# Splitting w2 by rows over fewer partitions, and a jump ahead in VectorE's program, in a decode step of attention and a feed-forward layer

## The chip, the cores and the metric

The kernel runs on one core of one Trainium2 chip. A core has five engines that run their own programs and meet at semaphores: TensorE (PE, matrix multiplication), VectorE (DVE), ScalarE (ACT), GpSimd (POOL) and SyncE (SP, which here only issues transfers). Sixteen DMA engines move data between the chip's memory (HBM) and the core's on-chip memory (SBUF, 128 partitions). The results of TensorE go to a second on-chip memory, PSUM. The metric is the device time of one execution in microseconds (us).

## The reference

One decode step for two sequences. Branch A is attention with 32 heads over a cache of 4096 keys and values, branch B is a feed-forward layer with 1376 hidden values; a gate mixes them. All tensors are bf16.

```python
# x (2,1,512), k_cache and v_cache (2,32,4096,128), wq (512,4096), wo (4096,512)
q = (x @ wq).reshape(B, Sq, 32, 128).transpose(0, 2, 1, 3)
scores = jnp.einsum("bhqd,bhkd->bhqk", q, k_cache) * (128 ** -0.5)
o = jnp.einsum("bhqk,bhkd->bhqd", softmax(scores), v_cache)
a = o.transpose(0, 2, 1, 3).reshape(B, Sq, 4096) @ wo
# w1 (512,1376), w2 (1376,512)
h = jnp.maximum(x @ w1, 0)
b = h @ w2
g = sigmoid((x * gate_w).sum(-1, keepdims=True))
return g * a + (1 - g) * b
```

Here x is the input A_x in both branches (B_x is not used): in the kernel xT3, its transposed copy, feeds wq and w1 alike.

The two caches are 64 MB each, so nearly all of the 145 MB that are read are keys and values.

## The kernel before

The order of each engine's work is written out by hand. `_Prog` collects operations for five lists (sp, pe, dve, act, pool) in the order of the calls; each names the markers it waits for and the one it signals. `emit` (line 61) then writes one engine's list straight through, with a wait instruction wherever a semaphore value is not known to have been reached.

Transfers: x and gate_w are issued by ScalarE (lines 265 and 266), everything else by SP in one sequence: w1 (267), wq (268), ten loads of keys (272), nine of values (282), wo in two parts (283, 284), then w2 (285 and 290), then one row of the output (295). A transfer of 128 partitions carries one contiguous row for each. A full load of keys or values is 8 MB, 64 KB for each partition; half loads are 4 MB. SP issues a load as soon as its buffer has been read, which it learns from the markers `kt_...` (VectorE has turned the last piece) or `pe_v_...` (TensorE has multiplied the last row).

The stages:

- `gate` computes the two gate factors; `selectors` makes small constant matrices; `q_proj` multiplies x by wq and `q_put` places the queries (ScalarE).
- `ffn_h` (line 370) computes the hidden values: TensorE multiplies 11 groups of 128 columns of w1 by x, four steps each, into PSUM; two VectorE operations (line 375, one for each sequence) apply the maximum with zero and the factor 1 - g and write `hT`. Group ft < 10 takes every tenth of the first 1280 columns, so that group r belongs to row r of a partition's ten rows of w2. Group 10 takes the columns 1248 to 1375, of which the first 32 have been used already; POOL sets those 32 partitions of hT to zero (line 379).
- 64 pieces of keys: VectorE transposes a piece (`k_turn`, line 386, 128x2048 as fp32), TensorE multiplies it by the queries (`k_scores`, lines 407 and 197).
- `softmax`, `denominators`, and `spread`, which lays the weights out for the values.
- nine units of values (`v_unit`, line 461), each followed by `v_extract` on VectorE (lines 467 and 471), which writes to `X2`.
- `o_gather` and `project` (wo, line 508), then `ffn_f` (line 516) and `wo_sum` (line 540). `ffn_f(r)` multiplies row r of w2 by hT in four column groups of 128 and adds to the same PSUM region `fin`. `ffn_last` does the last columns with weights loaded ahead (lines 202 and 208).
- VectorE and ScalarE copy the result to `out_sb` (lines 579 and 581), and SP and ScalarE send a row each.

w2 arrives in six transfers: row group 10 first (w2a: 128 partitions of one row, 1 KB), then the ten rows of each partition in columns 0 to 3071 (w2b), 3072 to 4351 (w2c) and three pieces of 256 columns (w2d, w2e, w2f), each with a semaphore of its own. `ffn_f(10)` runs first, then `wo_sum`, then rows 0 to 7 and the first half of 8, then `ffn_last`. The tiles w2 and X2 lie in `kt`, the buffer of the transposed keys.

## Time and profile before

| | us |
|---|---|
| median of three runs (344.19 to 344.23) | 344.23 |
| the profiled execution, first to last instruction (its span) | 342.9 |
| around the span, against the median | 1.3 |
| DVE busy | 178.5 |
| PE busy | 197.8 |
| ACT busy | 23.1 |
| POOL busy | 19.9 |
| HBM read | 145.46 MB, 424 GB/s over the span |

The profiled execution has no device time of its own besides its span. The profile's page gives the busy time of each engine, the share of the DMA engines in 40 slices of the span, the DMA queues by kind, the chain of waits that ended last, and the costliest groups of instructions by line of the kernel. In a group's row stand its busy time and the mean time of one, then the engine's idle time before it and what ended it. The trace behind the page also holds each DMA packet (start, duration, size, queue, but not which DMA engine moved it) and the time of each increment of a semaphore by a transfer: a transfer's semaphore goes up once for each DMA engine that has finished its share, 16 in all.

### The profile page before, as it was taken

What the parts mean: (1) busy time and instruction counts of PE and PEld (TensorE: products, weight loads), DVE (VectorE), ACT (ScalarE), POOL (GpSimd) and SP (SyncE); (2) the same over time, 40 slices, a digit from 0 to 9 for tenths busy, and PEclk for the clock granted to TensorE, in tenths of its full rate; (3) what the DMA queues carried; (4) which work ended last, traced back from release to release, by engine and by line L of the source; (5) the groups of instructions that cost most, each with busy time, mean ns of one, the idle gap of its engine ahead of it and who ended that gap; (6) DMA issues with size and microseconds to landing.
All of it is one profiled execution on the core that took longest, in us unless ns stands there. A gap on an engine that the chain in (4) does not pass through costs nothing.

```text
span 342.9 us, 2540 instructions
## 1 busy us (share of the span) xinstructions
PE 197.8 (58%) x1228; PEld 54.3 (16%) x972; DVE 178.5 (52%) x127; ACT 23.1 (7%) x71; POOL 19.9 (6%) x36
## 2 busy tenths in 40 slices
PE   0177329799969799699799337220706043150656
PEld 0141001111111111111111013100303011020231
DVE  2239059899789899698999562220100103020121
ACT  1040000000000000000000240000000000000000
POOL 8000000000000000000000040110100101000000
PEclk9999959989999999989999858755656756565787
DMA  8998989899998999999999999999999999998996
GB/s 348 428 489 369 482 375 482 382 474 413 438 489 367 429 443 466 392 459 390 475 420 436 461 390 420 445 466 413 443 413 445 428 428 443 413 468 382 440 401 239
DMA packets 4196, 145.61 MB, mean 425 GB/s; under 512 B 469, under 2 KB 986, under 8 KB 1242
## 3 DMA queue, kind: packets, MB, share of 16 engines
q1 hardware_dynamic: 4178, 145.46, 98.5%
q8 instruction: 8, 0.13, 0.2%
q14 instruction: 2, 0.02, 0.0%
q10 hardware_dynamic: 8, 0.00, 0.0%
HBM read 145.46 MB, written 0.00 MB: 424 GB/s over the span
## 4 chain that ended last, share of the span: by engine, by line
DMA 68%; DVE 15%; PE 13%; ACT 1%; issue 1%; POOL 0%; SPq 0%; DVEq 0%
DMA kv<-in_A_k_cache_dram 31%; DMA kv<-in_A_v_cache_dram 23%; DVE kt L386 13%; DMA kt<-in_B_w_dram 9%; PE PS L461 6%; DMA kv<-in_A_wq_dram 4%; PE PS L407 3%; PE PS L197 3%; ACT kt L428 1%; PE PS L333 1%; DVE mpad L413 1%; DVE kt L471 1%; POOL ptm L444 0%; DVE qbuf L467 0%; DVE kt L432 0%
## 5 line engine op out<-in xcount | busy, mean ns | idle before, releaser
L386 DVE STREAM_TRANSPOSE kt<-kv 128x2048 f32<-128x2048 f32 x64 | 141.2, 2274 | 22.4 <-DMA kv<-in_A_k_cache_dram 22.3
L407 PE MATMUL PS<-kt,qbuf 128*128 128x512 bf16 x256 | 105.7, 413 | 31.8 <-DVE kt L386 26.3
L197 PE MATMUL PS<-kt,qbuf 128*128 128x512 bf16 x256 | 105.1, 411 | 0.0
L461 PE MATMUL PS<-kv,ptm 128*32 128x512 bf16 x512 | 46.5, 541 | 79.0 <-DMA kv<-in_A_v_cache_dram 76.0
L467 DVE TENSOR_TENSOR qbuf<-PS,maskc 128x512 f32<-128x512 f32 x9 | 6.2, 692 | 109.0 <-PE PS L461 109.0
L407 PEld LDWEIGHTS PS<-kt,qbuf 128*128 128x128 bf16 x256 | 25.5, 100 | 139.9 <-DVE kt L386 72.7
L461 PEld LDWEIGHTS PS<-kv,ptm 128*32 128x32 bf16 x512 | 19.0, 129 | 105.1 <-issue 98.6
L444 POOL COPY ptm<-kt 32x512 bf16<-32x512 bf16 (+1 forms) x18 | 11.5, 638 | 268.7 <-DVE rsum L475 175.6
L360 ACT ACTIVATE qbuf<-PS 32x8 bf16<-32x8 bf16 x40 | 7.9, 196 | 134.2 <-PE PS L197 132.7
L448 ACT ACTIVATE ptm<-kt 32x512 bf16<-32x512 bf16 (+1 forms) x9 | 5.3, 603 | 100.1 <-PE PS L461 98.7
L471 DVE TENSOR_REDUCE kt<-qbuf 128x128 f32<-128x512 f32 x9 | 9.3, 1028 | 0.3
L428 ACT ACTIVATE kt<-PS,negm 128x512 bf16<-128x512 f32 x8 | 5.4, 696 | 30.4 <-DVE negm L424 30.4
L333 PE MATMUL PS<-kv,xTw 128*32 128x512 bf16 x32 | 3.6, 629 | 5.9 <-DMA kv<-in_A_wq_dram 5.9
L478 PE MATMUL PS<-rsum,sell 128*32 128x1 f32 x4 | 0.4, 196 | 10.1 <-DVE rsum L475 10.1
L432 DVE STREAM_TRANSPOSE kt<-kt 128x1024 bf16<-128x1024 bf16 x4 | 5.0, 1245 | 1.7 <-ACT kt L428 1.4
L348 DVE CAST qrow<-PS 128x256 bf16<-128x256 f32 x2 | 2.4, 1396 | 6.4 <-PE PS L333 6.4
L508 PE MATMUL PS<-kv,oW 128*2 128x512 bf16 x32 | 3.4, 590 | 1.4 <-DMA kv<-in_A_wo_dram 1.4
L300 PE MATMUL PS<-ident,x_sb 3*128 3x3 bf16 x4 | 0.3, 166 | 6.2 <-DMA x_sb<-in_gate_w_dram 6.2
L486 PE MATMUL PS<-kt,selx 128*32 128x128 f32 x18 | 3.4, 328 | 0.3 <-DVE kt L471 0.3
L303 DVE COPY xT<-PS 128x12 bf16<-128x12 bf16 x1 | 0.2, 169 | 6.5 <-PE PS L300 6.5
L230 POOL MEMSET ptm<- 128x4096 bf16 x1 | 3.5, 3501 | 0.0
L413 DVE TENSOR_REDUCE mpad<-PS 128x1 f32<-128x2048 f32 x1 | 2.3, 2290 | 2.1 <-PE PS L197 2.1
(64 smaller groups left out, 44.2 us busy)
## 6 DMA issues: line engine op xcount, KB each, us to landing
kv<-in_A_k_cache_dram SPq DMA_DIRECT2D x4, 4096.0 KB, 31.6
kv<-in_A_v_cache_dram SPq DMA_DIRECT2D x2, 4096.0 KB, 27.0
kv<-in_A_wq_dram SPq DMA_DIRECT2D x1, 4096.0 KB, 15.0
kv<-in_A_wo_dram SPq DMA_DIRECT2D x1, 3072.0 KB, 29.3
kt<-in_B_w_dram SPq DMA_DIRECT2D x1, 1376.0 KB, 5.8
kv<-in_A_wo_dram SPq DMA_DIRECT2D x1, 1024.0 KB, 31.3
kt<-in_B_w_dram SPq DMA_DIRECT2D x1, 768.0 KB, 31.9
kt<-in_B_w_dram SPq DMA_DIRECT2D x1, 320.0 KB, 32.3
```

Of the source, the lines that this page charges most:

```text
L197: return e.add_instruction(mybir.InstMatmult(start_tensor_calc=start, stop_tensor_calc=stop, tile_size=(128, 128), tile_position=(0, 0), l ...
L333: pe(lambda e, n=n, t=t: e.matmul(psf(32 * (n % 4), 32 * (n % 4) + 32, (QR_B + n // 4) * BANK, 512), lhsT=xTw[:, t, :], rhs=wq_sb[:, t, n ...
L360: act(lambda a, hq=hq: a.activation(out=qbuf[32 * hq:32 * hq + 32, g % 2, :, :, 32 + 32 * hq], in_=cols[32 * hq:32 * hq + 32, u4 // 2, 2 * ...
L386: dve(lambda v: v.transpose(out=dst, in_=pairs[:, h, 64 * rr:64 * rr + 64]), waits=([f"pe_sc_{i - NKT}"] if i >= NKT else ["pe_h"] if i == ...
L407: return e.matmul(args[0], lhsT=args[1], rhs=args[2], start=first, stop=last)
L413: dve(lambda v: v.tensor_reduce(out=mpad[:, 0:1], in_=psf(0, 128, 0, 2048), axis=AX.X, op=ALU.max), waits=["pe_sc_63", "c_mpad"], signal=" ...
L428: act(lambda a, bk=bk, e2=e2: a.activation(out=blocks[:, bk, :, 16 * e2:16 * e2 + 16], in_=psf(0, 128, bk * BANK, 512).rearrange("p (r n) ...
L444: pool(lambda e, args=args: e.tensor_copy(**args), waits=waits, signal=f"pt_{j}_{hq}")
L448: act(lambda e, args=args: e.activation(func=ACT.Copy, **args), waits=waits, signal=f"pt_{j}_{hq}")
L461: pe(lambda e, m=m, t=t: e.matmul(psf(32 * t, 32 * t + 32, V_B[j % 2] * BANK, 512), lhsT=ptm[:, j % 2, 4 * m:4 * m + 4, :, :], rhs=rows[:, ...
L467: dve(lambda e: e.tensor_tensor(out=Y.rearrange("p (c d) -> p c d", c=4), in0=psf(0, 128, V_B[u % 2] * BANK, 512).rearrange("p (c d) -> p ...
L471: dve(lambda e: e.tensor_reduce(out=X2[:, u, :], in_=Y.rearrange("p (c d) -> p d c", c=4), axis=AX.X, op=ALU.add), waits=[f"dve_y{u}"], si ...
```

## The change

w2 is cut otherwise. The first 1024 rows lie as 8 rows on each of 128 partitions, the next 320 as 5 rows on each of 64 partitions, the last 32 as 1 row on each of 32. No row is loaded twice. The 5 rows come by eight transfers of 8 partitions (every fourth partition of 32: 0, 4, ..., 28; 1, 5, ..., 29; and so on, then the same from 32), 5 KB for each partition; the last 32 rows by four transfers of 12, 10, 6 and 4 partitions. All twelve count up one semaphore, w2a, and stand where the one transfer of w2a stood; w2b to w2f follow with 2048, 1280 and three times 256 columns of the 8 rows.

`ffn_h` makes 14 groups: 8 of 128 columns, 5 of 64, 1 of 32. The zeroing on POOL goes; three VectorE operations (one for each width, both sequences at once) take the place of two. `ffn_f` does rows 8 to 13 first, after all twelve small transfers, then `wo_sum`, then rows 0 to 5 and half of 6; `ffn_last` does 6 and 7. The matmuls of the narrow groups use as many partitions as the group has. X2 is split into a tile of its own for units 0 to 4 and a part in kt for the rest; out_sb becomes two rows of x_sb.

VectorE's program is cut at its hundredth operation into two blocks with a third, `far`, between them in the program: a branch to `far`, where a no-op increments a semaphore that nobody waits for, a branch back to the first block (`near`), and at its end a branch over `far` to the rest (`on`).

```diff
-    def emit(self, engine, eng):
+    def emit(self, engine, eng, hop=None):
         seen = {}
-
+        ops = self.ops[engine]
+        if hop is None:
+            self.emit_part(engine, eng, ops, seen)
+            return
+        at, sem = hop
+        far, near, on = (f"{engine}_{n}" for n in ("far", "near", "on"))
+        only = [eng.engine]
+        eng.br(far)
+        with self.nc.body(near, valid_engines=only):
+            self.emit_part(engine, eng, ops[:at], seen)
+            eng.br(on)
+        with self.nc.body(far, valid_engines=only):
+            eng.nop().then_inc(sem, 1)
+            eng.br(near)
+        with self.nc.body(on, valid_engines=only):
+            self.emit_part(engine, eng, ops[at:], seen)
+
+    def emit_part(self, engine, eng, ops, seen):
...
-    hT = sb("hT", [128, 11, 2], dt.bfloat16)
-    out_sb = sb("out_sb", [2, 512], dt.bfloat16)
+    hT = sb("hT", [128, 14, 2], dt.bfloat16)
+    X2a = sb("X2a", [128, 5, 128], dt.float32)
+    out_sb = x_sb[0:2, :]
...
-    w2_in = B_w2[0:1280, :].rearrange("(p r) n -> p (r n)", r=10)
+    w2_in = B_w2[0:1024, :].rearrange("(p r) n -> p (r n)", r=8)
+    w2_mid = B_w2[1024:1344, :].rearrange("(p r) n -> p (r n)", r=5)
...
-    sp(lambda e: e.dma_start(w2[:, 10, :], B_w2[1248:1376, :]).then_inc(sem["w2a"], 16),
-       waits=[f"pt_8_{hq}" for hq in range(4)])
-
-
-    for name, c0, c1 in (("w2b", 0, 3072), ("w2c", 3072, 4352), ("w2d", 4608, 4864), ("w2e", 4352, 4608), ("w2f", 4864, 5120)):
+    ready = [f"pt_8_{hq}" for hq in range(4)]
+    few = [(w2f[b:b + 29:4, 4096:6656], w2_mid[b:b + 29:4, :]) for b in (0, 1, 2, 3, 32, 33, 34, 35)]
+    few += [(w2[p0:p1, 13, :], B_w2[1344 + p0:1344 + p1, :]) for p0, p1 in ((0, 12), (12, 22), (22, 28), (28, 32))]
+    for i, (dst, src) in enumerate(few):
+        sp(lambda e, dst=dst, src=src: e.dma_start(dst, src).then_inc(sem["w2a"], 16), waits=ready if i == 0 else [])
+    for name, c0, c1 in (("w2b", 0, 2048), ("w2c", 2048, 3328), ("w2d", 3584, 3840), ("w2e", 3328, 3584), ("w2f", 3840, 4096)):
...
+    def h_rows(r):
+        return 128 if r < 8 else 64 if r < 13 else 32
+
     def ffn_h():
-        for ft in range(11):
+        for ft in range(14):
...
-        pool(lambda g: g.memset(hT[0:32, 10, :], 0.0), waits=["dve_h0", "dve_h1"], signal="c_h10")
+        for i, (r0, r1) in enumerate(((0, 8), (8, 13), (13, 14))):
+            n = h_rows(r0)
+            dve(lambda v, r0=r0, r1=r1, n=n: v.scalar_tensor_tensor(
...
-        dw = {10: [(sem["w2a"], 16)], 0: [(sem["w2b"], 16)], 6: [(sem["w2c"], 16)]}.get(r, [])
+        dw = {8: [(sem["w2a"], 192)], 0: [(sem["w2b"], 16)], 4: [(sem["w2c"], 16)]}.get(r, [])
...
-    ffn_f(10, first=True)
+    ffn_f(8, first=True)
+    for r in range(9, 14):
+        ffn_f(r)
     wo_sum()
-    for r in range(8):
+    for r in range(6):
         ffn_f(r)
-    ffn_f(8, groups=2)
+    ffn_f(6, groups=2)
...
+    hops = {"dve": (100, nc.alloc_semaphore("dve_hop"))}
     P.resolve()
     for name, eng in (("sp", nc.sync), ("act", nc.scalar), ("pool", nc.gpsimd), ("pe", nc.tensor), ("dve", nc.vector)):
-        P.emit(name, eng)
+        P.emit(name, eng, hops.get(name))
```

## The prediction

> **What bounds the kernel now.** I read the page's 40 slices first, then the chain of waits, then busy time by stretches over the tail, then the tail's timeline, and last the packets and semaphore landings in the trace.

> ```profile
> DMA  8998989899998999999999999999999999998996
> q1 hardware_dynamic: 4178, 145.46, 98.5%
> q8 instruction: 8, 0.13, 0.2%
> q14 instruction: 2, 0.02, 0.0%
> ```

> The DMA engines have work in every slice until the last. Two rows matter for this change: eight fetches of instructions on q8 (16 KB each) and two on q14 (8 KB each).

> ```profile
> 308.17 32.26 DMA kt<-in_B_w_dram
> 340.43 0.04 issue
> 340.47 0.33 PE PS L516 x10
> 340.80 0.44 PE PS L208 x6
> 341.24 0.02 issue
> 341.27 0.28 DVE out_sb L579
> ```

> That is the end of the chain in order of time: it waits for w2 to land, then 0.84 us of work. So only the end of the DMA stream counts. By stretches (us, PE, PEld, DVE, ACT, POOL, clock, DMA share, GB/s) the stream does not end at once:

> ```profile
> 337.00:338.50 1.50, 1.50 (x20) 0.24 (x12) 0.02 (x1) 0.00 (x0) 0.00 (x0) 0.50 1.01 392
> 338.50:339.00 0.50, 0.04 (x4) 0.00 (x0) 0.50 (x1) 0.00 (x0) 0.00 (x0) 0.84 0.86 312
> 339.00:339.50 0.50, 0.28 (x8) 0.11 (x8) 0.17 (x1) 0.00 (x0) 0.00 (x0) 1.00 0.58 224
> 339.50:340.50 1.00, 0.66 (x35) 0.35 (x32) 0.00 (x0) 0.00 (x0) 0.00 (x0) 1.00 0.48 150
> ```

> In the last 1.5 us half of the 16 engines have nothing left. The last w2 transfer (semaphore w2f) lands once per engine: seven times between 339.09 and 339.64, once at 340.31, eight times between 340.78 and 340.97. Following each engine's packets back (one starts 4 ns before the last ends) shows why. Engines never pause from 1.77 us on, all carry the same bytes, and the ten instruction fetches fell on ten different engines. A 16 KB fetch pushes its engine back by 1.0 us of its own and some 0.5 us by which the next packet is stretched: 1.55 us, the eight heavy engines. The q14 fetch at 118.42 us cost its engine 0.93 us (the 340.31), that at 167.74 us 0.69 (the 339.64). The first comes 3.9 us after VectorE passed its 56th instruction, the second about 4 us after ScalarE passed its 46th, so I read them as VectorE's and ScalarE's next blocks of code.

> **The change part by part.** The sum runs on this execution: span 342.9 us, against a median of 344.23, so 1.33 us around it that I keep. What decides is the last landing of w2f, now 340.97.

> *Rows per transfer.* Packet durations (start to start is 4 ns less): 1024 B 46 ns, 2560 B 102, 6144 B 239, 8192 B 312. A kilobyte costs 37 to 39 ns, so 4096 B comes to 156 and 5120 B to 197 start to start. On every engine the old w2a goes (its landings stand 0.36 us behind those of wo1) and w2b's eight packets shrink from 6144 to 4096 B: 8 x (235-156) = 0.63. Both together -0.99 us. Engines that take the eight-row transfers get 8 packets of 5120 B with 8 semaphore packets (5 ns each beyond the overlap): 8 x 202 = 1.62. Row 13 comes in four transfers of 12, 10, 6 and 4 rows: at most 4 x 47 = 0.19. So an engine with small transfers gains 0.82 us of work, one without loses 0.99 to 0.89.

> *Which engines.* The profile numbers no engine. It does show that short transfers use few: the two rows of x are two packets that overlap (1.668 and 1.676 us), so two engines; the row of gate_w is one packet, at 5.238 us, and it sits in the only gap, 49 ns, of an engine that stayed light to the end. Of the six engines that got packets of w1 first, five are light of any 16 KB fetch. I take it that an eight-row transfer always goes to the same eight engines, first ones first, and that these are the eight without a 16 KB fetch. The bounds are both ends: all heavy, or all light.

> [...]

> *VectorE's hop.* Three branches and a no-op. The first runs at about 0.7 us, where VectorE has nothing until 6.47; if it stalls for the 4 us seen between cause and fetch it still ends by 5 us. The branch near the end of the stretch of V (operation 100) sits where VectorE waits for PE 109 us in nine times. Their own cost on the path is nothing, with that cover; without it, a few us once. What they can move is the q14 fetch of 118.42: to the first microseconds. Its price there is between 0 (before the first w1 packet at 1.77) and the 0.93 it costs now; nearest are the 0.31 to 0.33 of its own duration, since w1's packets of 11 KB leave less to stretch. I take 0.30.

> *Sum.* Heavy engines: 340.97-0.89 = 340.08 at most. Clean light ones: at most 339.47+0.82 = 340.29. ScalarE's: 339.64+0.82 = 340.46. VectorE's: 340.31-0.93+0.30+0.82 = 340.50. Last landing 340.50 instead of 340.97: **0.47 us earlier, 343.76**. With the hop free, 343.72; with its full 0.93, VectorE's engine lands at 341.13, 344.39.

> *The rest.* PE: 12 more pairs of load and matmul in ffn_h (2.60 us for 44, so 0.71) and three instead of two VectorE operations with POOL's memset gone (0.23 each): K's first transpose starts some 0.9 us later than 25.91. What is queued behind are K loads waiting for buffers, and each is issued over 9 us before the stream would run dry (that of 83.81 against the landing at 93.2). At the end PE's wait for w2a is for all twelve small transfers; behind it stand the first ffn_f rows and wo_sum. The latest of the twelve lands some 1.81 us after wo1 on its engine (8 x 202 and 4 x 47 ns): 336.0+1.81 = 337.8, before PE comes to it at 338.2. Then 24 instead of 4 matmuls stand ahead of wo_sum: 24 take 0.51 us, from 338.21 to 338.8, under VectorE's copy that ends at 339.17. Then 26 instead of 34 remain before the held ones; PE would be ready by 340.2, before w2f. The extra code (48 instructions of 2231) moves PE's fetches by 24 instructions, adds none before the data has landed. SP issues 17 transfers for 6: 11 x 0.43 = 4.7 us more, from 307.3 on, for data that moves after 334.8. Tail from w2f to the end unchanged: out_sb in x_sb's rows is read by nobody then.

> **The rivals.**

> *The eight are heavy* (ends slower). If small transfers fall on even one engine with a 16 KB fetch, that engine lands at 340.97+0.82 = 341.79: **345.05**. For: the profile numbers nothing. Against: gate_w's engine and the order of w1's first packets.

> *SP's queue runs dry* (slower). The fifth L290 issue:

> ```profile
> L290 SPq DMA_DIRECT2D kt<-in_B_w_dram x5: 432/432/8843, 307.7 to 309.6; - x5
> ```

> It stood 8.84 us, until V's second last load had landed at 317.83; then nine transfers were outstanding. If the limit counts transfers, the sixth small one waits for 317.83, the seventh for 327.5, two more for wo (334.9, 337.4), and w2b is issued at 339 and w2f at 340.9. With 1.04 us from issue to packet (0.73 to 1.77) and the rows above, w2f lands near 343.5: **346.7**. Against: a limit by packets fits as well. At 317.83 exactly 7 x 9 = 63 stood ahead (V's last, wo twice, w2a to w2d), and a small transfer puts only two on an engine; then all is issued by 337.

> *The hop adds instead of moving.* The early jump fetches, and the block at 118 us is fetched again: 340.31+0.30+0.82 = 341.43, **344.69**; with no effect at all 341.13, 344.39. [...]

> *More than that.* With every engine ending together the mean of the 16 landings, 340.17, is the floor for these bytes: 0.80 us, 343.4. ScalarE's and VectorE's engines stand against it.

> **How the numbers follow.** Works as summed, 343.4 to 344.05: 0.54. Hop without use or with a second fetch, 344.1 to 344.7: 0.16. Heavy engines: 0.13. SP's queue: 0.09. Near the floor: 0.08. Differences under 0.2% (0.69 us: 343.54 to 344.92) are about what a measurement of this kernel can tell from none. A quarter of the first case (0.14) and the last lie below: faster 0.22; the rest of the first and the hop: same 0.56; heavy engines and the queue: slower 0.22. The range 343.5 to 345.1 leaves out the queue and the parts below 343.5; the likeliest case alone is 343.5 to 344.05.

> **What would show it.** Right: DMA share above 0.8 until 340 and all landings of w2f within 0.6 us, the last near 340.5; one q14 packet before 7 us, none at 118; 64 packets of 5120 B on the engines without q8 packets. Wrong: a landing near 341.8 on an engine with a 16 KB fetch; L310's issues running past 330 us with the DMA share falling after 337; a second early q14 packet.

## The result: slower by 0.83 us

| | before | after |
|---|---|---|
| median of nine runs each, us | 344.23 (344.18 to 344.41) | 345.06 (344.91 to 345.41) |
| ratio, 95% interval | | 1.0022 (1.0013 to 1.0031) |
| profiled execution: span, us | 342.9 | 343.5 |
| last landing of w2f, us | 340.97 | 341.54 |

The forecast was 343.76, a little faster than before. The kernel became slower instead, by 0.2%: little, but all nine runs lie above all nine of the kernel before, and the interval lies clear of 1. The time is that of the rival "the eight are heavy" (345.05); how far that is more than luck is told in the part on the prediction.

The page of the changed kernel first: the 40 slices of the DMA engines' share, and the queues (packets, MB, share of 16 engines).

```profile
DMA  8998989999999999999999989999999989999995
q1 hardware_dynamic: 4226, 145.43, 98.4%
q8 instruction: 9, 0.15, 0.2%
q14 instruction: 2, 0.02, 0.0%
```

Still full until the last slice. There is one more fetch on q8, at 341.30 us, after the data of all but one engine had landed. The two fetches on q14 are still two; the packet records put them at 3.22 and 167.57 us, before it was 118.42 and 167.74. The jump of VectorE did what its code says.

The end of the chain of waits of the changed kernel, in order of time:

```profile
314.74 26.16 DMA kt<-in_B_w_dram
340.90 0.04 issue
340.94 0.33 PE PS L544 x10
341.27 0.55 PE PS L226 x6
341.82 0.02 issue
341.84 0.28 DVE x_sb L609
```

The same shape as before, half a microsecond later: PE waits for w2 to land, then the tail. PE's last matmul ends 0.28 us after the last landing of w2f (341.54 to 341.82; before 0.27). So in this execution the DMA stream still sets the end. By stretches (us, PE, PEld, DVE, ACT, POOL, clock, DMA share, GB/s):

```profile
337.00:338.50 1.50, 1.50 (x20) 0.27 (x12) 0.00 (x0) 0.00 (x0) 0.00 (x0) 0.56 0.99 367
338.50:339.00 0.50, 0.15 (x4) 0.00 (x0) 0.29 (x1) 0.00 (x0) 0.00 (x0) 1.00 0.90 340
339.00:339.50 0.50, 0.00 (x0) 0.00 (x0) 0.40 (x1) 0.00 (x0) 0.00 (x0) 1.00 0.87 282
339.50:340.50 1.00, 0.99 (x48) 0.77 (x48) 0.00 (x0) 0.00 (x0) 0.00 (x0) 1.00 0.29 93
340.50:341.50 1.00, 0.72 (x26) 0.28 (x16) 0.07 (x1) 0.07 (x1) 0.00 (x0) 1.00 0.11 26
```

Between 339.0 and 339.5 the share rose from 0.58 to 0.87: the split does even out most engines. But in the last microsecond a share of 0.11 is left, under two engines of sixteen. The 16 landings of w2f say which:

```
before  7 from 339.09 to 339.64, 340.31, 8 from 340.78 to 340.97
after   338.56 338.61   11 from 339.93 to 340.38   340.87 341.11 341.54
```

Two engines end a whole microsecond too early, eleven end together where they should, and three are late. To see who they are, each engine's packets were followed from the end of wo1 (every engine's packets follow one another within a few ns), and the engines told apart, and numbered, by how many packets of 5120 B and of 1 KB they moved (the marker runs below show that n rows went to n engines, each set inside the next larger one): the transfers of 12, 10, 6 and 4 rows leave engines 0 to 3 with four of 1 KB, 4 and 5 with three, 6 and 7 with two, 8 and 9 with two, 10 and 11 with one. From wo1's end to w2f's end an engine with small transfers took 4.42 to 4.52 us, one without 2.69 to 2.83; before, every engine took 3.63 to 3.65. The one latest and the one at 341.11 are of the first kind, and each carries a 16 KB fetch (at 303.38 and at 324.74 us), one of them engine 4 or 5, the other engine 6 or 7. The two at 338.6 are of the second kind and carry no fetch: they were relieved for nothing.

### The profile page after: what moved, and what is told of

The parts are those of the page before. It is cut to its first block, busy times and chain, and to the rows that moved or that the text cites. A ratio compares the mean times of both kernels' runs of the same rounds, so it can differ in the third digit from the quotient of the medians.

```text
span 343.5 us, 2603 instructions
## 1 busy us (share of the span) xinstructions
PE 198.9 (58%) x1252; PEld 55.4 (16%) x996; DVE 178.7 (52%) x128; ACT 23.1 (7%) x71; POOL 19.8 (6%) x35
## 4 chain that ended last, share of the span: by engine, by line
DMA 66%; DVE 19%; PE 10%; SPq 2%; ACT 1%; issue 1%; POOL 0%; DVEq 0%
DMA kv<-in_A_k_cache_dram 31%; DMA kv<-in_A_v_cache_dram 22%; DVE kt L410 16%; DMA kt<-in_B_w_dram 8%; PE PS L485 7%; DMA kv<-in_A_wq_dram 5%; SPq L308 2%; ACT kt L452 1%; PE PS L431 1%; PE PS L215 1%; PE PS L353 1%; DVE mpad L437 1%; POOL ptm L468 0%; DVE qbuf L494 0%; DVE kt L456 0%
## 5 line engine op out<-in xcount | busy, mean ns | idle before, releaser
L498 DVE TENSOR_REDUCE X2a<-qbuf 128x128 f32<-128x512 f32 x5 | 5.1, 1029 | 0.2
L498 DVE TENSOR_REDUCE kt<-qbuf 128x128 f32<-128x512 f32 x4 | 4.1, 1021 | 0.1
L394 PE MATMUL PS<-xT,kt 128*128 128x2 bf16 (+2 forms) x56 | 3.9, 202 | 0.0
L394 PEld LDWEIGHTS PS<-xT,kt 128*128 128x128 bf16 (+2 forms) x56 | 3.8, 166 | 0.0
```

What stands on the lines that cost most here:

```text
L394: return e.matmul(psf(0, h_rows(ft), H_C0 + 2 * ft, 2), lhsT=w1[:, o + c0:o + c1:step], rhs=xT3[:, t, 0:2], start=(t == 0), stop=(t == 3))
L498: dve(lambda e: e.tensor_reduce(out=x2(u), in_=Y.rearrange("p (c d) -> p d c", c=4), axis=AX.X, op=ALU.add), waits=[f"dve_y{u}"], signal=f ...
```

## The experiments

The theory from these rows: engines 0 to 7 get the small transfers, and two of them carry a 16 KB fetch; these two set the end. Rivals: the jump of VectorE is what costs; a narrow transfer costs a fixed time, whatever its bytes; PE, which now comes to its first FFN rows at 339.50 instead of 338.2 because it waits for all twelve small transfers, ends last; the engines that carry the fetches are others in each execution.

### Numbering the engines, first attempt (two single executions)

The kernel before, with w2a as sixteen transfers of different numbers of rows, so that each engine gets its own number of packets:

```diff
-    sp(lambda e: e.dma_start(w2[:, 10, :], B_w2[1248:1376, :]).then_inc(sem["w2a"], 16), ...)
+    for i, n in enumerate((8, 15, 14, 13, 12, 11, 10, 9, 8, 7, 6, 5, 4, 3, 2, 1)):
+        sp(lambda e, p0=p0, n=n: e.dma_start(w2[p0:p0 + n, 10, :], B_w2[1248 + p0:1248 + p0 + n, :]).then_inc(sem["w2a"], 16), ...)
+        p0 += n
```

> The kernel before, with w2a's 128 rows sent by sixteen transfers of 8, 15, 14, ... 1 partitions in place of one. An engine's place among the sixteen is then read from the number of 1 KB packets it moves. Theory 1 (a transfer of n partitions takes the n first engines, and the eight 16 KB fetches fall on a mixture of first and last engines, at least one among the first eight): packet counts 16, 15, ... 9, 7, ... 0, and at least one of the engines with 9 or more carries a 16 KB fetch; the last landing of w2f lies between 340.6 and 341.4 against 340.97, as the first engine gets 8 packets more (0.38 us). Rival (all eight fetches on the last eight engines, and something else made the changed kernel late): every engine with 9 or more packets is free of 16 KB fetches.

> The same kernel once more, to see whether the fetches keep their engines. Theory 1a (fixed by the block of code): the k-th fetch falls on the same engine as in the first look. Rival 1b (the engine moves on from one execution to the next): the set of engines with fetches is another one, and the time of the changed kernel spreads by up to 0.8 us with it while that of the kernel before does not.

Measured: 345.70 and 345.51 us. As a numbering they failed: packets of 6144 B took up to 915 ns, of 8192 B up to 422 (commonly 234 and 311), so the engines' chains could no longer be told apart. The last landings of w2f, 342.38 and 342.19, lie far above the 340.6 to 341.4 forecast from the bytes. The bytes in all are those of before, and the kernel lost 1.3 to 1.5 us: something other than bytes can cost here. That came back below.

### The two halves of the change apart

After without the jump, and before with the jump:

```diff
 after without the jump:
-    hops = {"dve": (100, nc.alloc_semaphore("dve_hop"))}
+    hops = {}
 before with it (emit and emit_part as in the change):
+    hops = {"dve": (100, nc.alloc_semaphore("dve_hop"))}
-        P.emit(name, eng)
+        P.emit(name, eng, hops.get(name))
```

> The changed kernel without VectorE's hop. Theory 1 (an engine that has both a 16 KB fetch and the small transfers sets the end; last landing 341.5): VectorE's fetch comes back to about 118 us, its engine lands some 0.4 us later than with the hop (0.93 us for 0.5), at 341.2 to 341.4, still before 341.5: time 345.0 to 345.2, no change against the changed kernel's 345.06. Rival (the hop makes the loss): back to 344.2 to 344.5. Other rival (VectorE's engine is the last): 345.4 to 345.6.

> The kernel before with the hop alone. Theory 1: one q14 fetch near 3.2 us and none near 118; VectorE's engine carries no 16 KB fetch and does not set the end, so 344.2 to 344.3, no change. Rival (the hop makes the loss): 344.8 or more.

| | median, us | ratio to before | last landing of w2f |
|---|---|---|---|
| without the jump | 345.00 (344.95 to 345.30) | 1.0023 (1.0014 to 1.0033) | 341.46 |
| the jump alone | 344.27 (344.06 to 344.50) | 1.0002 (0.9993 to 1.0012) | 340.93 |

The whole loss is the split's, and the jump gains or loses no more than 0.1%. Without the jump there are again exactly two engines with small transfers and a 16 KB fetch, again one of 4 and 5 and one of 6 and 7. The fetches on them are others: those of 87.9 and 136.2 us, the second and third, where it was the seventh and eighth in after. Which fetch an engine takes moves from execution to execution; that two of the low eight get one did not.

One thing is different at the end of the profiled execution without the jump. TensorE's granted clock stayed at 0.50 there, where after had 1.00 from 338.50 on, and from the landing of the small transfers at 339.35 TensorE had work up to its last matmul:

```profile
312.47 26.88 DMA kt<-in_B_w_dram
339.35 0.04 issue
339.39 0.90 PE PS L544 x24
340.29 0.54 PE PS L568 x8
340.83 0.73 PE PS L544 x26
341.56 0.12 PE PS L226 x4
```

```profile
339.50:340.50 1.00, 1.00 (x32) 0.60 (x28) 0.00 (x0) 0.00 (x0) 0.00 (x0) 0.50 0.27 90
340.50:341.50 1.00, 1.00 (x38) 0.83 (x32) 0.00 (x0) 0.00 (x0) 0.00 (x0) 0.50 0.09 26
```

The second copy of the result began at 342.02, 0.55 us after the last landing of w2f (341.46), where it was 0.30 in before and in after. So here TensorE ended last, as the rival has it, but that is worth only about 0.2 us of this execution's time. In after TensorE had 0.28 us to spare. What set the clock in the one execution and the other no run shows.

Why the jump gains nothing shows at the other end of the trace. The landings of w1 on the 16 engines, in executions with the early fetch and without (us):

```
                 VectorE's fetch at, took    w1: median   last
before           118.42, 333 ns              6.32         6.49
without the jump 118.27, 333 ns              6.12         6.58
after              3.22, 309 ns              6.33         7.00
jump alone         3.56, 307 ns              6.15         7.34
nine rows          3.12, 795 ns              6.12         7.17   (an experiment below)
four engines       3.84, 307 ns              6.11         7.62   (an experiment below)
```

With the early fetch one engine is 0.7 to 1.5 us behind the median, without it 0.2 to 0.5: the fetch at 3 to 4 us meets the first packets of w1 and wq (11 and 32 KB). At 118 us it had cost 0.93. It was moved and not made cheaper. The end of the stream agrees: without the jump VectorE's engine landed at 340.98, not at the 341.2 to 341.4 forecast, and so only 0.11 us later than with it (340.87).

### Numbering the engines, with markers (two single executions)

The kernel before, with fifteen tiny transfers of 15, 14, ... 1 rows ahead of w2a, each with a row size of its own. An engine's markers stop at the number that gives it away.

```diff
+    mark = flat[:, 4096:6144].bitcast(dt.bfloat16).rearrange("p (n c) -> p n c", c=256)
+    for n in range(15, 0, -1):
+        sp(lambda e, n=n: e.dma_start(mark[0:4 * n - 3:4, n, 0:64 + 4 * n], B_w2[0:n, 0:64 + 4 * n]).then_inc(sem["mark"], 16), ...)
```

> The kernel before with fifteen tiny transfers of 15, 14, ... 1 rows (each row size its own, 68 to 124 elements, partitions four apart so that no packets go to neighbours) ahead of w2a; the engine that gets all fifteen is engine 0, the one that gets none engine 15, so the trace tells which engine carries which instruction fetch. Theory (the set is uneven): two of the eight 16 KB fetches fall on engines 0 to 7, one on engine 4 or 5 and one on 6 or 7; six on engines 8 to 15; engines 0 to 3 carry none. Rival (before, the fetches lie on the high eight, and the split of w2 moved them): eight on engines 8 to 15. Time: 344.3 to 344.6, some 0.05 to 0.4 us of extra packets.

> The same kernel again. Theory: the same eight engines carry the 16 KB fetches, and the order in which they take them may differ. Rival (where a fetch goes is left to chance): another set of eight engines.

The markers of one engine follow one another every 16 to 20 ns, and every chain could be read. The 15 transfers left one packet for each row, 120 in all; they run from one engine that got all fifteen to one that got none. So n rows, from 1 to 15, went to n engines, each set inside the next larger one. The numbers below are given by the markers: engine 0 got all fifteen, engine 15 none. Engine, and the fetch that its chain holds:

```
engine   first execution        second execution
0 2 4    none                   none
1        ScalarE's, 167.7       ScalarE's, 167.8
3        VectorE's, 118.3       VectorE's, 119.3
5        16 KB at 217.4         16 KB at 216.4
6        16 KB at 264.5         16 KB at 265.0
7 8 15   none                   none
9 to 14  16 KB, one each        16 KB, one each
```

The times were a miss: 345.35 and 345.56 instead of 344.3 to 344.6. By stretches, the first of the two (columns as above):

```profile
336.00:337.00 1.00, 1.00 (x16) 0.15 (x4) 0.00 (x0) 0.00 (x0) 0.00 (x0) 0.50 0.98 277
337.00:338.50 1.50, 1.17 (x12) 0.13 (x8) 0.29 (x1) 0.00 (x0) 0.00 (x0) 0.57 1.04 334
```

and the same of the kernel before:

```profile
336.00:337.00 1.00, 1.00 (x16) 0.29 (x8) 0.00 (x0) 0.00 (x0) 0.00 (x0) 0.50 0.96 383
337.00:338.50 1.50, 1.50 (x20) 0.24 (x12) 0.02 (x1) 0.00 (x0) 0.00 (x0) 0.50 1.01 392
```

The engines are as busy as ever and move 277 instead of 383 GB/s: the packets behind the markers take longer. A 1 KB packet of w2a took up to 725 ns (commonly 46), a 6144 B packet of w2b up to 1079 (commonly 235).

### Five eighths of the bytes

As after, with nine rows on 128 partitions and three on 64: the same twelve small transfers, with packets of 3 KB.

```diff
-    w2_in = B_w2[0:1024, :].rearrange("(p r) n -> p (r n)", r=8)
-    w2_mid = B_w2[1024:1344, :].rearrange("(p r) n -> p (r n)", r=5)
+    w2_in = B_w2[0:1152, :].rearrange("(p r) n -> p (r n)", r=9)
+    w2_mid = B_w2[1152:1344, :].rearrange("(p r) n -> p (r n)", r=3)
```

> As after, but nine rows on 128 partitions, three on 64 by the same eight transfers of 8 rows, one on 32: the same count of transfers, packets of 3072 B instead of 5120 B. Theory (the bytes of the small transfers on an engine that also carries a 16 KB fetch set the end): such an engine gets -0.36 -0.31 + 8 x 0.124 + 0.19 = +0.51 us instead of +0.82, so five eighths of the loss of after: 344.7 to 344.8, the last landing of w2f near 341.3. Rival (each small transfer costs a fixed time, whatever its bytes): 345.0, as after. Rival (PE's later start on the narrow rows sets the end): below 344.5, with w2f landed before 341.1.

Measured: 345.09 us, ratio 1.0024 (1.0014 to 1.0034), last landing 341.77. That is the rival's number, and the theory's was missed. The two latest landings, 341.73 and 341.77, are again engines with small transfers and a 16 KB fetch, but their last part took about 4.49 and 4.72 us where the bytes alone give 4.1: the eight packets of w2b on them, 5120 B each, took up to 485 ns instead of 196, in all 0.40 and 0.58 us more. So the bytes were saved and another cost came in their place. Two runs followed to see which of the narrow transfers brings it: half as many of them with the same bytes (192 rows as six rows on 32 partitions, four transfers of 8), and the eight without the four of 12, 10, 6 and 4 rows, which leaves the last 32 rows of w2 out of the result. The cuts below are against the kernel with nine rows.

```diff
 half as many:
+    w2n = flat[0:32, 4096:5888].bitcast(dt.bfloat16)
-    few = [(w2f[b:b + 29:4, 4608:6144], w2_mid[b:b + 29:4, :]) for b in (0, 1, 2, 3, 32, 33, 34, 35)]
+    few = [(w2n[b:b + 29:4, 0:3072], w2_mid[b:b + 29:4, :]) for b in range(4)]
 without the four:
-    few += [(w2[p0:p1, 12, :], B_w2[1344 + p0:1344 + p1, :]) for p0, p1 in ((0, 12), (12, 22), (22, 28), (28, 32))]
```

> As the run with nine rows on 128 partitions, with the same bytes per engine, but the 192 rows as six rows on 32 partitions by four transfers of 8 (48 KB) instead of eight of 24 KB; the last 32 rows by the same four of 12, 10, 6 and 4. There the two latest engines showed 0.5 to 0.6 us of stretched packets of w2b. Theory A (the number of narrow transfers stretches what follows): the stretch goes, heavy engines with small transfers land at 340.97 - 0.67 + 4 x 0.24 + 0.14 = 341.4 or below: 344.6 to 344.75. Theory B (the four transfers of 1 KB packets stretch it): as there, landing at 341.7, 345.0 to 345.1.

> As the run with nine rows on 128 partitions and eight transfers of 24 KB, but without the four transfers of 12, 10, 6 and 4 rows: the last 32 rows of w2 are left out of the computation. Theory A (the number of narrow transfers stretches what follows): eight are left, most of the stretch stays, landing at 341.5 to 341.65: 344.85 to 345.0. Theory B (the transfers of 1 KB packets stretch it): the stretch goes, landing at 340.97 - 0.67 + 8 x 0.124 = 341.3 or below: 344.4 to 344.65.

| | median, us | ratio to before | last landing | stretch in all |
|---|---|---|---|---|
| twelve narrow transfers | 345.09 | 1.0024 (1.0014 to 1.0034) | 341.77 | 4.7 us |
| four of 8 and four | 344.68 (344.44 to 345.44) | 1.0015 (1.0006 to 1.0024) | 341.34 | 1.0 us |
| eight of 8 alone | 344.63 (344.34 to 345.71) | 1.0013 (1.0004 to 1.0023) | 341.31 | 0.3 us |

(Stretch: by how much the packets of SP's queue between 333 and 342 us took longer than the commonest duration of their size, summed over the 16 engines; counted from 15 ns on.) In both runs the stretch is nearly gone, and the time is then what the bytes alone give: landings of 341.34 and 341.31 against 341.4 and 341.3 worked out, times inside the two ranges of "the stretch goes". The medians alone do not tell bytes from number, since both runs also have eight narrow transfers for the twelve of after. The engines' own times from wo1 to w2f do. Eight packets of 3 KB added 0.97 to 1.04 us to an engine (3.93 to 4.00 us against 2.96, one stretched engine 4.08), eight of 5 KB in after about 1.6 (4.42 to 4.52 against 2.74, with 0.05 us taken off for each packet of 1 KB), and four of 6 KB 0.93 to 0.97 (4.08 to 4.21 against 3.05, less the same): three fifths of the bytes cost about three fifths of the time, in eight packets or in four. So the bytes on an engine that also carries a fetch price the loss, and a fixed time per transfer is out. What brings the stretch is not settled: taking away either kind of transfer took it away, and after, with the same twelve, has 1.0 us of it.

### Away from the fetches

If the theory holds, small transfers on engines 0 to 3 alone leave no engine with both them and a 16 KB fetch. Ten rows on 128 partitions as before, 96 rows as six rows on 16 partitions by four transfers of 4 partitions, with the jump:

```diff
+    w2n = flat[0:16, 4096:5632].bitcast(dt.bfloat16)
+    few = [(w2n[b:b + 13:4, :], w2_mid[b:b + 13:4, :]) for b in range(4)]
```

> With the hop; ten rows on 128 partitions as before, the last 96 rows as six rows on 16 partitions by four transfers of 4 partitions each (24 KB), so that only four engines get small transfers. Theory (engines 0 to 3 carry no 16 KB fetch): those four do 4 x 0.24 - 0.36 = 0.6 us more and end below 340.5; all others lose the 0.36 us of w2a, the heavy ones land near 340.61: 343.87, range 343.75 to 344.05, a little faster than before. Rival (a 16 KB fetch falls on one of the four in some executions): 340.97 + 0.6, 344.8. Rival (24 narrow matmuls ahead of wo_sum make PE the last): 344.2 or more with w2f landed by 340.7.

Measured: 344.36 us (344.03 to 344.53), ratio 1.0003 (0.9994 to 1.0012): the loss is gone, and the hoped-for gain did not come. Landings of w2f: four from 338.74 to 339.05, 339.59 and 339.64, nine from 340.15 to 340.45, and one at 341.18. The nine landed at least 0.16 us sooner than the 340.61 worked out for the heavy engines, without any stretched packet (0.00 us). The one is an engine with small transfers that came late to them. I take it for VectorE's: its w1 landed 1.5 us behind the median after the early fetch at 3.84 us (the table above), and it also got the 0.58 us of small transfers. The packets do not settle this. VectorE's engine and the one that carried the 16 KB fetch at 184.8 us end packets within 1 ns of each other several times between 212 and 293 us, so the two can be exchanged, and the rival "a 16 KB fetch falls on one of the four" would give the same landing. For VectorE's speaks that its fetch lay on engine 3 in both marker runs, and that no 16 KB fetch lay on engines 0 to 3 there, nor in after, without the jump, half as many and nine rows. The chain of waits of this run:

```profile
308.67 31.92 DMA kt<-in_B_w_dram
340.59 0.04 issue
340.64 0.33 PE PS L543 x10
340.97 0.49 PE PS L226 x6
341.46 0.02 issue
341.48 0.28 DVE x_sb L609
```

PE ran 24 narrow matmuls ahead of wo_sum here and was in time all the same: its end is 0.28 us after the last landing. The rival "PE ends last" is out for this kernel.

So engines 0, 1 and 2 alone, without the jump: 96 rows as four rows on 24 partitions by eight transfers of 3 partitions, eight apart in one run and four apart in the other.

```diff
+    w2n = flat[0:24, 4096:5120].bitcast(dt.bfloat16)
 eight apart:
+    few = [(w2n[b:b + 17:8, :], w2_mid[b:b + 17:8, :]) for b in range(8)]
 four apart:
+    few = [(w2n[b:b + 9:4, :], w2_mid[b:b + 9:4, :]) for b in (0, 1, 2, 3, 12, 13, 14, 15)]
```

> Without the hop; ten rows on 128 partitions, the last 96 rows as four rows on 24 partitions by eight transfers of 3 partitions (12 KB each), so that only engines 0, 1 and 2 get small transfers; by the two marker runs the 16 KB fetches lie on engines 5, 6 and 9 to 14, ScalarE's 8 KB on engine 1 and VectorE's on engine 3. Theory: engines 0 and 2 end at 339.47 - 0.36 + 8 x 0.161 = 340.4, engine 1 at 339.64 + 0.93 = 340.57, VectorE's engine at 340.31 - 0.36 = 339.95, the eight heavy ones at 340.97 - 0.36 = 340.61: 343.87, range 343.75 to 344.05. Rival (a narrow transfer stretches the packets behind it, as in the run with 3 KB packets): up to 0.5 us more on three engines, 344.2 to 344.4. Rival (the set of engines is another in other executions): 344.6 or more in some of them.

> As the run with three engines, whose packets of w2 were stretched by up to 0.2 us each on all engines between 335.3 and 337.7 us; here the three partitions of one transfer lie four apart instead of eight (0, 4, 8 and so on, as in the runs that were not stretched), and the source rows 16 KB apart instead of 32. Theory A (the distance within a transfer makes the stretch): it goes, the heavy engines land at 340.6, engine 1 at 340.57: 343.87, range 343.75 to 344.05. Theory B (three engines with eight narrow transfers each make the stretch at any distance): 344.4 to 344.7 with the last landing near 341.0.

Measured: 344.55 us, ratio 1.0010 (1.0001 to 1.0019), and 344.98 us, ratio 1.0021 (1.0012 to 1.0030). The first run's three engines carried no 16 KB fetch, as the markers had said. Both times miss 343.87, and they lie above the rivals' ranges for a stretch too (344.2 to 344.4, and 344.4 to 344.7). The stretch was 7.9 and 10.4 us over the 16 engines, and it fell on all of them: nearly all of those without small transfers took 3.57 to 3.84 us from wo1 to w2f in the first of the two, against 3.25 to 3.28 with four engines. The distance of the partitions within a transfer is not its cause. By stretches, three engines eight apart:

```profile
339.50:340.50 1.00, 0.53 (x28) 0.34 (x32) 0.00 (x0) 0.00 (x0) 0.00 (x0) 0.80 0.59 182
340.50:341.50 1.00, 0.82 (x16) 0.36 (x16) 0.36 (x2) 0.37 (x2) 0.00 (x0) 0.50 0.06 17
```

and four engines:

```profile
339.50:340.50 1.00, 0.51 (x24) 0.32 (x24) 0.00 (x0) 0.00 (x0) 0.00 (x0) 1.00 0.36 98
340.50:341.50 1.00, 0.80 (x16) 0.28 (x16) 0.30 (x2) 0.29 (x2) 0.00 (x0) 1.00 0.01 4
```

With four engines the share between 339.5 and 340.5 is 0.36 and only one engine is left after it (0.01); with three it is 0.59: the late work is that of many engines. None of the versions here is faster than the kernel before.

## Why the prediction was wrong

Point by point, by its own steps.

**The bound.** Right, with one exception. The time follows the last landing of w2f:

```
                       last landing   profiled execution   difference
jump alone             340.93         344.28               3.35
three engines          341.01         344.47               3.46
four engines           341.18         344.46               3.28
eight of 8 alone       341.31         344.59               3.28
half as many           341.34         344.67               3.33
three, four apart      341.43         344.73               3.30
without the jump       341.46         344.98               3.52
after                  341.54         344.91               3.37
nine rows              341.77         345.09               3.32
```

The four numbering executions have 3.32 each. The two above 3.4 have a later second copy of the result: 0.55 us after the last landing without the jump, where TensorE ended last, and 0.40 with three engines, against 0.30 to 0.35 in all others. The prediction's "PE would be ready by 340.2, before w2f" held no term for a granted clock of 0.50.

**Rows per transfer.** Right, within 0.1 us. An engine with small transfers was to gain 0.82 us of work and gained 0.77 to 0.88 (4.42 to 4.52 us against 3.64); one without was to lose 0.99 to 0.89 and lost 0.81 to 0.95. The packets themselves cost their bytes and the four-byte packet, as the line through the sizes said: 50 of the 64 of 5120 B took 196 ns, 30 of the 37 of 1 KB 46 ns. What came on top is the stretch of the packets behind them, 1.0 us over 16 engines in after, up to 14.0 in others.

**Which engines.** This step failed, and with it the forecast: it put the small transfers on engines without a 16 KB fetch, so that the last landing would be 340.50. Two engines had both, and the later of them landed at 341.54. "I take it that an eight-row transfer always goes to the same eight engines, first ones first, and that these are the eight without a 16 KB fetch": the first half holds, the second does not. In the marker runs the eight without a 16 KB fetch are 0 to 4, 7, 8 and 15; the small transfers go to 0 to 7, so by them engines 5 and 6 carry both, and 8 and 15 carry neither. The step rested on two hints that were true and too weak: gate_w's engine is one engine, and "of the six engines that got packets of w1 first, five are light" says that the sixth is not. The rival gave 341.79 for an engine with both and took the latest heavy engine's landing as its start. The two that met are earlier ones: 336.58 and 337.07 at the end of wo1, where the latest of before stood at 337.36. The later one came 0.29 us earlier and gained 0.86 us instead of 0.82, which is the 0.25 us between 341.79 and the 341.54 measured. That the median of 345.06 still meets the rival's 345.05 is luck: the profiled execution took 344.91, with 3.37 us behind the last landing where the sum kept 3.26, and the median lies 0.15 us above it.

**VectorE's hop.** The mechanism held: no fetch at 118 us, one near 3 us (3.22 in after), no second one. The rival "the hop adds instead of moving" is refuted. The price was mis-sized: 0.30 taken, between 0 and 0.93, because "w1's packets of 11 KB leave less to stretch". Measured, by the landings of w1: 0.7 to 1.5 us behind the median, from inside the range to well above it. In after VectorE's engine landed at 340.87 instead of 340.50; it did not decide there, but without the two engines that did, the time would have been about 344.13 and not 343.76. With four engines it probably decided. The other fetches have their price too: in before one of 16 KB put 1.55 us on one of 16 engines in a stream that sets the time.

**The rest.** The wait for w2a was put too early: 337.8 forecast, 339.46 measured. Part of it is that a late engine's small transfers also come late: the last narrow packet ended at 338.31 us. The rest is the semaphore. Its last increment came 1.15 us behind that packet, while those of w2f came 0.4 to 0.7 us behind theirs; the prediction had no such term. Its consequence was small in this execution: from 339.50 PE ran 24 and 16 matmuls and wo_sum, and it still stood idle 0.28 us for w2c's landing at 340.90. SP's issues: 0.43 us each assumed, 0.62 to 0.76 measured for eight rows and 0.30 to 0.47 for the last four transfers; these are the groups of the twelve and of w2b to w2f (duration in ns min/median/max, first and last start):

```profile
L308 SPq DMA_DIRECT2D kt<-in_B_w_dram x12: 295/623/761, 307.3 to 314.0; - x12
L310 SPq DMA_DIRECT2D kt<-in_B_w_dram x5: 355/2200/7847, 314.3 to 325.3; - x5
```

**SP's queue runs dry.** Refuted. Eighteen transfers stood ahead of w2d when it was let in at 317.4 us (V's last two, two of wo, twelve small ones, w2b, w2c), where before nine stood ahead of the fifth issue, which stood 8.84 us. So what held the issues back (in after 2.20, 7.85 and 6.39 us for w2d, w2e and w2f) was not the number of transfers; whether it was the number of packets was not tested. w2f, the last, was issued by 331.7 us (325.34 + 6.39), six microseconds ahead of its data.

**The chances.** 0.13 stood on what happened. Its first argument was "the profile numbers nothing", and it needed but one heavy engine among eight: with eight heavy of sixteen and two weak hints that was too little.

## What to carry to other kernels

Where all DMA engines are busy to the end, work out which engine each transfer and each instruction fetch lands on before shifting bytes between engines: a fetch of 16 KB made one engine 1.55 us late here, and a split that spares the late half on average still loses if one late engine gets more. An unnumbered trace can be numbered with a few marker transfers of different row counts and sizes. And look at the durations of the packets behind a series of narrow transfers, not only at the narrow ones: their bytes were priced right, and what came with them raised the time by 1.3 to 1.5 us in two executions that moved the bytes of before. A wait moved to a later semaphore also uses up another engine's slack, which a lower granted clock can turn into time, as in the run without the jump (clock 0.50, the second copy of the result 0.55 us after the last landing, where it was 0.30 in after).

## What the hardware showed unexpectedly

Packets behind narrow transfers were stretched in most of these runs, on engines that move the same bytes without a pause. Stretch as defined above, summed over the engines:

```
                    narrow transfers                         stretch, us
before              none                                     0.2
four engines        4 of 4 rows, 6 KB                        0.0
eight of 8 alone    8 of 8 rows, 3 KB                        0.3
half as many        4 of 8 rows, 6 KB, and 4 of 1 KB         1.0
after               8 of 8 rows, 5 KB, and 4 of 1 KB         1.0
without the jump    the same                                 1.4
nine rows           8 of 8 rows, 3 KB, and 4 of 1 KB         4.7
three engines       8 of 3 rows, 4 KB, eight apart           7.9
three, four apart   8 of 3 rows, 4 KB, four apart            10.4
markers             15 of 15 to 1 rows, 136 to 248 B         12.3 and 12.4
first numbering     16 of 15 to 1 rows, 1 KB                 13.3 and 14.0
```

In this list the stretch was larger with more narrow transfers (4.7 us with twelve in nine rows, 0.3 with its eight alone), with fewer bytes in them (4.7 with 3 KB, 1.0 with 5 KB in after) and with fewer engines (7.9 with eight transfers of 4 KB on three, 0.3 with eight of 3 KB on eight); no single one of these orders the list. In the marker runs it sits on the first packets behind the markers (1 KB in up to 725 ns, 6144 B in up to 1079); the cause was not tested and stays open.

The semaphore of narrow transfers also trailed their packets. It did not go up 16 times for a transfer as that of w2f did: in after w2a went up 12 times from 308.46 to 314.47 us, once for each issue, and 96 times from 335.54 to 339.46, once for each row. The first of the 96 increments of w2a came about 0.55 us behind the packets, the last 1.15 us; with nine rows the last came 1.6 us behind, with eight of 8 alone 1.2. The increments of w2f kept to 0.4 to 0.7 in these kernels. Why was not tested.

The issue of a narrow transfer to every fourth partition took SP longer than that of a wide one: 623 ns for eight rows in after and 732 for the markers' median, against 327 to 434 for 128 rows in before. The narrow transfers to neighbouring partitions were not slower: 465 to 295 ns for 12 to 4 rows, 379 to 252 in the first numbering. And the 16 KB fetches kept to engines 5, 6 and 9 to 14 in both marker runs, while in after, without the jump, half as many and nine rows there was one on 4 or 5 and one on 6 or 7 each time, with the fetch that takes a given engine moving from run to run.
